# Moving a nested product's steps forward in a Strassen-type feed-forward kernel

## The chip, the cores and the metric

The kernel runs on one core of one Trainium2 chip. The metric is device time in microseconds of one execution. TensorE is called PE here, its weight loads PEld, VectorE DVE, ScalarE ACT, GpSimd POOL and SyncE SP.

## The reference

Hash attention is followed by a feed-forward block. In shapes: q, k, v are (4, 8, 768, 64) and the weights are (512, 2048) and (2048, 512).

```python
mask = q_bucket[:, :, :, None] == k_bucket[:, :, None, :]
scores = np.where(mask, scale * np.matmul(q, k.transpose(0, 1, 3, 2)), -1000000000.0)
attn = softmax(scores); x = (attn @ v), heads joined   # (3072, 512)
h = x @ w_in                                            # (3072, 2048)
g = np.maximum(h, 0.0) + alpha * np.minimum(h, 0.0)
out = g @ w_out                                         # (3072, 512)
```

The four batches of 768 tokens each go through the feed-forward block one after the other.

## The kernel before, in words

The attention of all batches comes first, in 16 pairs of heads, and prepares sums of the weights beside it. Then the feed-forward block runs for batches 0 to 3. A batch has a **stage 1** (h and g, eight blocks `ff1(b, 0)` to `ff1(b, 7)`) and a **stage 2** (out, seven blocks `ff2(b, 0)` to `ff2(b, 6)`). Both multiply by a seven-product scheme of Strassen's kind: a matrix is cut in quarters (0, 1, 2 and 21 or 12), sums and differences of quarters are made (3 to 6), and seven products of such sides, added up in the right order, give the four quarters of the result. `SIDES` and the steps of `Product.step` are numbered by product: 1 is (0, 0), 2 is (1, 1), 5 is (3, 3), 6 is (4, 4), 3 is (6, 2), 7 is (5, 5), 4 is (2, 6).

In stage 1 a block is one product scheme: PE accumulates groups in PSUM banks a, b and c, ACT copies partial sums out (`p1`, `p5`, `u1`, `u2`, `h`) or copies a start value into a bank (a "seed"), DVE adds and applies the slope, and so writes g. From batch 1 on a block is a `Rest`: its products 1, 5 and 2 are not made on their own, but come from products that are nested once more and serve four blocks at once (a **unit**; a batch has units 0 and 1, of blocks 0 to 3 and 4 to 7). The class `Inner` makes two of them, called `one` (outer product 1) and `two` (outer product 5), in the function `unit`, before the unit's first block. The class `Third` makes the nested product for outer product 2; its seven steps are spread over the blocks by the table `THIRD`, whose keys are (block in the unit, place in the block). In the profile, PE groups of `Inner` and `Third` have the line L1122 and names n: na, nb, nc belong to `one`, nd, ne, nf to `two`, n_2a, n_2b, n_2c to `Third`. A step with a or d as output works on the product's running bank. Groups of the blocks have the line L928 and names f_0a, f_0c and so on; those of stage 2 z_1a, z_1b, z_1c, by product number in `ORDER`.

What each name does in the later steps:

- `sum_g(count)` (L977) takes `count` entries from the list `g_due`, in which `finish` in `ff1` puts the four differences g3, g5, g4, g6, in that order, for the rows that are complete. Stage 2 uses g0 in its block 0, g1 in block 1, g3 in 2, g4 in 3, g2 in 4, g5 in 5 and g6 in 6. In the kernel before, rows 0 to 5 are summed in pairs of blocks (128x768), rows 6 and 7 one by one (128x384), and all of them within stage 1.
- `sum_w2` (L1334) makes the weight sums ws3 to ws6 of a stage 2 product from a loaded tile wl, `sum_g2` (L1342) the sums gs3 to gs6 of its g side. ws5 and ws6, like gs5 and gs6, have one buffer and share it with copies that `Inner` and `Third` keep.
- `sum_inner(b, u, o)` (L1091) works in batch 1 only: four sums of weights for a nested product, each stored by a POOL DMA for the later batches. `load_third` (L1073, L1083) loads them on SP.
- `load_w2` (L1302) loads wl on SP; there are two buffers, so that a load waits for the product two earlier.
- `turn_out` (L1389, L1396) transposes finished output and stores it.

PSUM: tags b and c have one bank each, shared by units, blocks and stage 2; `two_banks` has three buffers, for the a banks and some c banks. A buffer comes free when its last reader has finished. The kept copies u1 and u2 of the blocks have one buffer each too.

The order on every engine is the order in which the program is written: `do` keeps it. DMAs on SP outside of `do` may be moved by the compiler. In the loop, a block's turn begins with its product 2 (`now.step(2)`, nothing for a `Rest`), and goes on with its later products; product 1 of the next block, or for a `Rest` its products 6 and 5, comes ahead of the last product of the block before:

```python
now = after
now.step(6)
third(b1, n1, "6")
now.step(5)
before.step(4)
third(b1, n1, "4")
```

Of the kernel before, what the change touches and what calls it, by code (L numbers as in the profile page):

```python
# [407 lines left out]
def fast_path(  # L408
# [460 lines left out]
    x_m, w_m, g_m = {}, {}, {}  # L869
    H2, HK, HC = DM // 4, NI // 2, CW // 2  # L870
# [112 lines left out]
    def ff1(b, i):  # L983
        whole = b == 0

        def finish(c, t, more):
            if more is None:
                h = mid.tile([P, CW], F32, name=f"h{b}_{i}", tag="h")
                do(ACT.copy(h, t))  # L989
            else:  # L990
                h = t
                do(DVE.tensor_tensor(h, t, more, op=ALU.add))

            al = slope(i, c[0] == "2")
            m = {"11": 0, "21": 1, "22": 2, "12": 5}[c]
            do(DVE.scalar_tensor_tensor(new_g(b, m)[:, i], h, al, h, op0=ALU.mult, op1=ALU.max))  # L996
            if c == "21" and (whole or i % 2 or i > 5):
                at = slice(i if whole or i > 5 else i - 1, i + 1)
                for x in ((3, 5, 0), (5, 2, 5), (4, 2, 3), (6, 1, 4)):
                    g_due.append((b, at, *x))  # L1000
            if whole or i > 5:
                sum_g(len(g_due))
            elif c in ("12", "21"):
                sum_g(1)

        w = w_m[b * NI + i]
        kind, seeded = (Product, ("b",) if i else ()) if whole else (Rest, ("a", "c"))
        made = kind(
            f"f{b}_{i}", CW, 2, lambda m, k: w[m][:, k], lambda m, k: x_m[b, m][:, k], finish, seeded=seeded,
        )  # L1010
        if not whole:
            made.p1, made.p5 = (n_s[b, i // 4, o, i % 4 // 2][:, i % 2] for o in range(2))
        return made
# [26 lines left out]
    n_w, n_x, n_s = {}, {}, {}  # L1040
# [45 lines left out]
    def sum_inner(b, u, o):  # L1086

        if b != 1:
            return
        for m, x, op, y in ((3, 21, ALU.add, 2), (4, 3, ALU.subtract, 0), (5, 0, ALU.subtract, 21), (6, 1, ALU.subtract, 4)):  # L1090
            do(DVE.tensor_tensor(n_w[b, u, o, m], n_w[b, u, o, x], n_w[b, u, o, y], op=op))  # L1091
            nc.gpsimd.dma_start(w_n_s[u, o, :, m - 3].rearrange("p (t f) -> p t f", t=2), n_w[b, u, o, m])
# [79 lines left out]
    class Third(Inner):  # L1172

        def __init__(self, b, u):
            self.key, self.o, self.seeded = (b, u, 2), 2, True
            self.name = f"n{b}_{u}_2"
            self.ps, self.sb = {}, {}

        TAG = {"p5": "p5", "u1": "p1", "u2": "gs6"}

# [52 lines left out]
                self.slopes(1)  # L1233

    thirds = {}
    THIRD = {(0, "3"): 1, (0, "7"): 2, (1, "6"): 6, (1, "4"): 5, (1, "3"): 7, (1, "7"): 3, (2, "6"): 4}

    def third(b, i, place):

        n = THIRD.get((i % 4, place))  # L1240
        if n:
            if n == 1:
                thirds[b, i // 4] = Third(b, i // 4)
            thirds[b, i // 4].step(n)

    def unit(b, u, before):

        def bank(name, tag=None):
            name = f"n{name}{b}_{u}"
            return psum_bc[0].tile([P, 512], F32, name=name, tag=tag) if tag else two_banks(name)[:, 0]  # L1250

        one = Inner(b, u, 0, bank("a"), bank("b", "b"), bank("c"))
        one.step(1)
        one.step(5)
        before.step(4)
        one.step(2)
        if not u:
            sum_inner_x(b, 1)
        one.step(6)
        if not u:  # L1260
            sum_inner(b, 0, 1)
            sum_x(b, 3, DVE)
        two = Inner(b, u, 1, bank("d"), bank("e", "b"), bank("f", "c"))
        two.step(1)
        one.step(3)
        two.step(5)
        one.step(7)
        two.step(2)
        two.step(6)
        one.step(4)  # L1270
        two.step(3)
        now = ff1(b, 4 * u)
        now.step(1)
        two.step(7)
        now.step(6)
        now.step(5)
        two.step(4)
        if u:
            sum_w2(b, 0, 3, 4, 6, 5)
        turn_out()  # L1280
        if not u:
            sum_inner_x(b, 2)
        sum_inner(b, u, 2)
        return now

    def new_g(b, m):
# [39 lines left out]
    def sum_w2(b, n, *ms):  # L1326

        if n < 7:
            for m in ms:
                x, op, y = {  # L1330
                    3: (21, ALU.add, 2), 4: (3, ALU.subtract, 0), 5: (0, ALU.subtract, 21), 6: (1, ALU.subtract, 4),
                }[m]
                w2[b, n, m] = t = late[0].tile([P, HK, H2], F32, name=f"ws{b}_{n}_{m}", tag=f"ws{m}", bufs=1 + (m < 5))
                do(DVE.tensor_tensor(t, w2[b, n, x], w2[b, n, y], op=op))  # L1334
# [157 lines left out]
    for pi in range(NPAIR):  # L1492
        i = 2 * pi
# [93 lines left out]
    for j, (b, what, n) in enumerate(blocks):  # L1587
        n2 = n + 1 if what == "2" else 0 if n == NI - 1 else 7
        if n2 == 0:
            sides_g(b, 0)  # L1590
            if b == 0:
                sum_w2(b, 0, 3, 4)
        if not j:
            now.step(6)
        elif not (b and what == "1"):
            now.step(2)
        if j == 0:
            now.step(3)
            now.step(7)
            now.step(2)  # L1600
        if what == "2" and n == 6 and b + 1 < B:
            sum_inner(b + 1, 0, 0)
        now.step(22)
        if (b, what, n) == (1, "2", 1):
            largest()
        if what == "2" and b + 1 < B and 2 <= n < 6:
            if n == 3:
                sum_inner_x(b + 1, 0)
            else:
                sum_x(b + 1, {2: 0, 4: 1, 5: 2}[n], DVE)  # L1610
        if b and what == "1" and n == 1:
            load_inner(b, 1)
        if b and what == "1" and n == 2:
            load_third(b, 1)
        if b and what == "1" and n in (2, 3):
            sum_inner(b, 1, n - 2)
        if 0 < n2 < 7:
            sides_g(b, n2)
            sum_w2(b, n2, 3, 4)
        if n2 < 7:  # L1620
            sum_g2(b, n2, 3, 4)
        if j:
            if not (b and what == "1"):
                now.step(5)
                now.step(6)
            now.step(3)
            if b and what == "1":
                third(b, n, "3")
            if n2 or b == 0:
                sum_w2(b, n2, 6)  # L1630
            if b and what == "1" and (n + 1) % 4:
                after = ff1(b, n + 1)
                after.step(1)
            now.step(7)
            if b and what == "1":
                third(b, n, "7")
            if n2 or b == 0:
                sum_w2(b, n2, 5)
            sum_g2(b, n2, 5)
        if (b, what, n) == (1, "2", 3):  # L1640
            verdict()

        for n_out in [(), (0,), (1,), (2, 3), (4,), (5, 6), (7,)][j] if j < 7 else ():
            sum_out(n_out)
        for n_out in [(1,), (2, 3), (4,), (5, 6), (7,)][j] if j < 5 else ():
            load_out(n_out)
        if what == "1":
            load_w(b * NI + n + 3)

            if b and n in (2, 5):  # L1650
                load_w2(b, n // 4)
            if not b and n >= NI - 2:
                load_w2(b, n - NI + 2)
        else:
            load_w2(b, n + 2)
            if b + 1 < B:
                if n == 5:
                    load_inner(b + 1, 0)
                    load_third(b + 1, 0)
                if n == 0:  # L1660
                    load_x(b + 1)
        if j + 1 == len(blocks):
            turn_last(0)
        elif what == "1" or n < 6:
            turn_out()
        before = now
        if j + 1 < len(blocks):
            b1, what1, n1 = blocks[j + 1]
            if b1 and what1 == "1" and n1 % 4 == 0:
                now = unit(b1, n1 // 4, before)  # L1670
            elif b1 and what1 == "1":
# [6 lines that stand above are left out]
            else:  # L1678
                now = ff1(b1, n1) if what1 == "1" else ff2(b1, n1)
                now.step(1)  # L1680
                before.step(4)
        else:
            before.step(4)
        if n2 < 7:
            sum_g2(b, n2, 6)
# [29 lines left out]
```

## Time and profile before

| what | value |
|---|---|
| median of three runs | 870.87 us |
| range | 870.1 to 871.62 us |
| profiled execution | 870.79 us |
| its span, first to last instruction | 868.9 us |
| PE, DVE, ACT, POOL busy | 850.8, 773.6, 407.5, 154.2 us |
| granted PE clock, mean | 0.998 |

A batch's stage 1 takes about 70 us and its stage 2 about 64 us in batches 1 to 3 (stage 1 of the last batch runs from 722.5 to 792.5). PE's groups in stage 1 have four matmuls, of 384 columns (L928) or 192 (L1122), in stage 2 eight of 192. In a timeline, a row is: start in us from the start of the span, duration, engine, line, operation, out<-in with its shape, how many were merged, and in brackets the idle time before it with what ended it. Durations overlap a little with the next start, so the time that a row costs is read from start to start.

### The profile page before, as it was taken

Reading aid. Unit: us, or ns where it says so; the run is one execution under the profiler, and the core shown is the slowest. Engines: PE = TensorE matmul, PEld = TensorE weight load, DVE = VectorE, ACT = ScalarE, POOL = GpSimd, SP = SyncE. Lnnn points to the kernel's source line nnn. Section 1 sums busy time; section 2 is a strip of 40 time slices with the busy share of each in tenths; the row PEclk is TensorE's granted clock in tenths of the full one; section 3 lists DMA queues with packets and bytes.
Section 4 is the critical chain, followed back from the end, with each engine's and each line's share of the span. In section 5 each row is a group of like instructions: output and inputs, shape, how many; then the busy total and the mean of one; then the engine's idle time right before and its main releaser. Section 6 shows DMA issues by size and latency. Waiting matters only on the chain.

```text
span 868.9 us, 15379 instructions
## 1 busy us (share of the span) xinstructions
PE 850.8 (98%) x5674; PEld 598.5 (69%) x5674; DVE 773.6 (89%) x1263; ACT 407.5 (47%) x754; POOL 154.2 (18%) x321
## 2 busy tenths in 40 slices
PE   9999999999999999999999999999999999999996
PEld 4444444444444445569997768998767998677996
DVE  6999999999999977899997899996889997869886
ACT  7777888878788823321124441114442113452111
POOL 1322423333433310210015100003000001200000
PEclk9999999999999999999999999999999999999999
DMA  8856879889697537774355633444833335720242
GB/s 199 192 131 132 208 177 235 171 202 236 133 265 196 158 131 246 249 257 157 119 167 174 238 117 108 129 154 135 304 114 123 118 107 182 284 98 1 98 164 60
DMA packets 181765, 144.85 MB, mean 167 GB/s; under 512 B 121536, under 2 KB 161648, under 8 KB 178096
## 3 DMA queue, kind: packets, MB, share of 16 engines
q1 hardware_dynamic: 166496, 113.15, 45.5%
q0 software_dynamic: 12176, 29.29, 11.2%
q10 hardware_dynamic: 3008, 1.33, 0.6%
q8 instruction: 47, 0.77, 0.4%
q14 instruction: 38, 0.31, 0.1%
HBM read 111.16 MB, written 31.46 MB: 164 GB/s over the span
## 4 chain that ended last, share of the span: by engine, by line


## 5 line engine op out<-in xcount | busy, mean ns | idle before, releaser
L790 ACT ACTIVATE pt<-sc 128x768 f32<-128x768 f32 x192 | 153.9, 812 | 3.3 <-PE sc L787 3.0
L787 PE MATMUL sc<-qT,kT 64*128 64x384 f32 x768 | 155.1, 482 | 0.0
L820 PE MATMUL av<-pt,vn 128*32 128x385 f32 (+1 forms) x1536 | 127.0, 485 | 0.0
L820 PEld LDWEIGHTS av<-pt,vn 128*32 128x32 f32 x1536 | 50.3, 109 | 73.9 <-issue 69.3
L787 PEld LDWEIGHTS sc<-qT,kT 64*128 64x128 f32 x768 | 68.3, 187 | 37.7 <-issue 37.5
L1396 POOL DMA_DIRECT2D out_dram<-o x52 | 28.2, 551 | 340.6 <-DVE o L1389 339.1
L977 DVE TENSOR_TENSOR g<-g,g 128x384 f32<-128x384 f32 (+1 forms) x92 | 63.9, 710 | 1.1
L787 PE MATMUL sc<-qb,kb 64*128 64x384 bf16 x384 | 63.1, 323 | 0.8 <-DVE alpha L563 0.5
L1342 DVE TENSOR_TENSOR gs<-g,gs 128x768 f32<-128x768 f32 x56 | 53.3, 951 | 1.0
L1342 DVE TENSOR_TENSOR gs<-g 128x768 f32<-128x768 f32 x56 | 53.2, 951 | 0.0
L1334 DVE TENSOR_TENSOR ws<-wl 128x512 f32<-128x512 f32 x56 | 38.4, 685 | 7.6 <-DMA wl<-w_out_s 7.5
L787 PEld LDWEIGHTS <-kb 64*128 64x128 bf16 x384 | 19.5, 94 | 34.9 <-issue 11.9
L607 ACT ACTIVATE wr<-raw 128x512 int32<-128x512 uint32 x32 | 22.1, 691 | 30.0 <-DVE wso L651 15.2
L798 DVE TENSOR_TENSOR accp<-pt,pt 128x1536 f32<-128x1536 f32 x16 | 28.1, 1757 | 7.3 <-ACT pt L790 7.3
L748 POOL DMA_DIRECT2D qb<-hr x60 | 30.0, 506 | 25.7 <-ACT hr L743 25.7
L996 DVE SCALAR_TENSOR_TENSOR g<-h,alpha 128x384 f32<-128x384 f32 x39 | 23.9, 613 | 7.1 <-ACT h L989 7.1
L803 DVE TENSOR_TENSOR accd<-accd,pt 128x1536 f32<-128x1536 f32 x16 | 28.1, 1758 | 1.7
L809 DVE TENSOR_TENSOR accd<-accd,accp 128x1536 f32<-128x1536 f32 x16 | 28.1, 1758 | 0.6
L806 DVE TENSOR_TENSOR accp<-accp,pt 128x1536 f32<-128x1536 f32 x16 | 28.1, 1754 | 0.0
L802 DVE TENSOR_TENSOR accd<-pt,pt 128x1536 f32<-128x1536 f32 x16 | 28.0, 1751 | 0.0
L1546 ACT ACTIVATE qT<-qT 128x768 f32<-128x768 f32 x15 | 12.7, 845 | 25.8 <-DMA kb<-hr 19.0
L1354 DVE TENSOR_TENSOR m<-m,m 128x768 f32<-128x768 f32 x24 | 22.7, 946 | 0.3
(494 smaller groups left out, 1903.7 us busy)
## 6 DMA issues: line engine op xcount, KB each, us to landing
wi<-w_in_s SPq DMA_DIRECT2D x32, 512.0 KB
wl<-w_out_s SPq DMA_DIRECT2D x16, 1024.0 KB
wl<-w_out_r SPq DMA_DIRECT2D x12, 1024.0 KB
raw<-in_moe_w_in_dram POOLq DMA_DIRECT2D x15, 512.0 KB, 5.0
raw<-in_moe_w_out_dram POOLq DMA_DIRECT2D x14, 512.0 KB, 4.9
w_in_s<-wsi SPq DMA_DIRECT2D x16, 448.0 KB
qn<-in_q_dram SPq DMA_DIRECT2D x64, 96.0 KB
vn<-in_v_dram SPq DMA_DIRECT2D x16, 384.0 KB
```

Source lines behind the costliest of these rows:

```text
L748: queue.dma_start(bits[name, pi][D * s : D * s + 2 * NB, half * CW : (half + 1) * CW], raw[c : c + 2 * NB],)
L787: do(PE.matmul(sc[:, s, :CW], what["k", pi][r, ks], what["q", pi][r, qs], start=first, stop=not first,))
L790: do(ACT.activation(pts[kc][:, g, :, :CW], sc[:, :, :CW], AF.Exp, scale=SCALE / DOWN))
L798: do(DVE.tensor_tensor(accp[pi], p(0), p(1), op=ALU.add))
L803: do(DVE.tensor_tensor(accd[pi], accd[pi], p(5), op=ALU.add))
L806: do(DVE.tensor_tensor(accp[pi], accp[pi], p(2), op=ALU.add))
L809: do(DVE.tensor_tensor(accd[pi], accd[pi], accp[pi], op=ALU.add))
L820: do(PE.matmul(av[pi][D * s + t : D * s + t + 32, g, :w], nat["v", pi][:, s, kc * D + t : kc * D + t + 32], pts[kc][:, g, s, :w], start=(k ...
L977: do(DVE.tensor_tensor(new_g(b, to)[:, at], g_m[b, x][:, at], g_m[b, y][:, at], op=ALU.subtract))
L1334: do(DVE.tensor_tensor(t, w2[b, n, x], w2[b, n, y], op=op))
L1342: do(DVE.tensor_tensor(t, g2[b, n, x], g2[b, n, y], op=ALU.subtract))
L1396: pinned(b + 1 < B and queue is nc.sync, queue.dma_start(out_v[b, ch * CH + c].rearrange("(w r) d -> r w d", r=32)[:, :, cols], src[32 * a ...
```

## The change

Five edits, in the code of batches 1 to 3:

1. The `Third` object is made in `unit`, and some of its steps are called there. In unit 0, step 1 stands at the end of `unit`, ahead of the first block's product 3. In unit 1, step 1 follows `two.step(6)`, step 2 follows `two.step(3)`, and step 6 follows `two.step(4)`. `THIRD` becomes a table for each unit, with the other steps: in unit 0, step 2 moves from place "7" of the first block to place "3", where step 1 was, and the rest stay; in unit 1, steps 5 and 7 are in the first block, 3 and 4 ahead of the second.
2. `Third` gets a first `n_x` with the two unsummed quarters, since step 1 in unit 0 now stands ahead of `sum_inner_x(b, 2)`.
3. In unit 1, `sum_inner(b, 1, 2)` (batch 1) and `sum_w2(b, 0, 3, 4)` move from the end of `unit` to after `one.step(7)`; `sum_w2(b, 0, 6, 5)` stays at the end.
4. Rows 6 and 7 of g's sums are treated as a pair, and `sum_g` takes one entry at a time there too.
5. So three of the last four sums are left at the end of stage 1: `sum_g(1)` takes one in block 0 of stage 2 and `sum_g(2)` two in block 1.

The numbers and shapes of matmuls, and every DMA, are as before.

```diff
-            if c == "21" and (whole or i % 2 or i > 5):
-                at = slice(i if whole or i > 5 else i - 1, i + 1)
+            if c == "21" and (whole or i % 2):
+                at = slice(i if whole else i - 1, i + 1)
...
-            if whole or i > 5:
+            if whole:
                 sum_g(len(g_due))
             elif c in ("12", "21"):
                 sum_g(1)
...
+            n_x.setdefault((b, 2), {k: x_m[b, 1][:, k, :HC] for k in range(2)})
...
-    THIRD = {(0, "3"): 1, (0, "7"): 2, (1, "6"): 6, (1, "4"): 5, (1, "3"): 7, (1, "7"): 3, (2, "6"): 4}
+    THIRD = (
+        {(0, "3"): 2, (1, "6"): 6, (1, "4"): 5, (1, "3"): 7, (1, "7"): 3, (2, "6"): 4},
+        {(0, "3"): 5, (0, "7"): 7, (1, "6"): 3, (1, "4"): 4},
+    )
...
-        n = THIRD.get((i % 4, place))
+        n = THIRD[i // 4].get((i % 4, place))
         if n:
-            if n == 1:
-                thirds[b, i // 4] = Third(b, i // 4)
             thirds[b, i // 4].step(n)
...
         one.step(7)
+        if u:
+            sum_inner(b, 1, 2)
+            sum_w2(b, 0, 3, 4)
         two.step(2)
         two.step(6)
+        three = thirds[b, u] = Third(b, u)
+        if u:
+            three.step(1)
         one.step(4)
         two.step(3)
+        if u:
+            three.step(2)
         now = ff1(b, 4 * u)
         now.step(1)
         two.step(7)
         now.step(6)
         now.step(5)
         two.step(4)
+        three.step(6 if u else 1)
         if u:
-            sum_w2(b, 0, 3, 4, 6, 5)
+            sum_w2(b, 0, 6, 5)
         turn_out()
         if not u:
             sum_inner_x(b, 2)
-        sum_inner(b, u, 2)
+            sum_inner(b, 0, 2)
         return now
...
+        if what == "2" and n < 2:
+            sum_g(1 + n)
```

## The prediction

> **What bounds the kernel now.** I read the page, then the waits of TensorE, then the timelines of PE, DVE and ACT around each wait. The run from which all durations come took 870.79 us: a span of 868.9 and 1.9 around it, 0.08 below the median of the runs, 870.87. Three runs lie within 0.2%, so a change under 0.2% could not be told from none.
>
> From the page:
>
> ```profile
> span 868.9 us, 15379 instructions
> ...
> PE 850.8 (98%) x5674; PEld 598.5 (69%) x5674; DVE 773.6 (89%) x1263; ACT 407.5 (47%) x754; POOL 154.2 (18%) x321
> ```
>
> TensorE's own stream is the bound; time can be won only where it waits. The view of waits (total, times, longest):
>
> ```profile
> PE z_1c L928 <- DVE f_7u L992: 3.4, 3, 1.1
> PE z_2c L928 <- DVE m L1363: 1.6, 3, 0.5
> ...
> PE f_3c L928 <- ACT f_3c L1020: 1.0, 1, 1.0
> PE f_4c L928 <- ACT f_4c L1020: 0.9, 3, 0.3
> PE f_0c L928 <- ACT f_0c L1020: 0.9, 3, 0.3
> ```
>
> Four of the five come once in each of batches 1 to 3. The PE timeline, last batch, where columns are start, duration, what:
>
> ```profile
> 768.39 0.81 PE L1122 MATMUL nd<-xn,wq 128*128 128x192 f32 x4
> 769.51 1.56 PE L928 MATMUL f_4c<-x,wi 128*128 128x384 f32 x4 [0.30 <-ACT f_4c L1020]
> 770.90 0.81 PE L1122 MATMUL n_2a<-x,wt 128*128 128x192 f32 x4
> ...
> 795.06 1.46 PE L928 MATMUL z_1b<-g,wl 128*128 128x192 f32 x8
> 797.67 1.57 PE L928 MATMUL z_1c<-gs,ws 128*128 128x192 f32 x8 [1.14 <-DVE f_7u L992]
> 799.08 1.46 PE L928 MATMUL z_1a<-gs,ws 128*128 128x192 f32 x8
> ```
>
> Unhindered starts lie 0.65 us apart (n), 1.29 (f), 1.30 (z). So a wait costs more than its label: f_4c comes 0.46 late and its successor another 0.11, 0.57 together (f_0c the same); z_1c 1.31 + 0.11 = 1.42; z_2c (805.58 to 807.55 to 808.96) 0.67 + 0.11 = 0.78; f_7c (788.35 to 789.79 to 791.18), whose wait has no label, 0.15 + 0.10 = 0.25. The DVE timeline says why z_1c is late:
>
> ```profile
> 793.08 2.20 DVE L977 TENSOR_TENSOR g<-g,g 128x384 f32<-128x384 f32 x4
> 795.21 0.95 DVE L1342 TENSOR_TENSOR gs<-g 128x768 f32<-128x768 f32 x1
> 796.19 0.96 DVE L1342 TENSOR_TENSOR gs<-g,gs 128x768 f32<-128x768 f32 x1
> 797.07 0.55 DVE L992 TENSOR_TENSOR f_7u<-f_7u,f_7c 128x384 f32<-128x384 f32 x1
> ```
>
> z_1c takes f_7c's PSUM bank (tag c, one buffer), and DVE reads f_7c only after g's sums. It still trails at z_2c, which needs z_1c's bank.
>
> [...] the trace has 0.95 and 0.55, so two half sums cost more than one whole.
>
> **The change, part by part,** on the last batch's clock with its second unit starting as before. Pitches (start to start) are from the DVE rows: L992 0.58, L996 0.54, pair sum L977 0.87, L1196 0.47 (0.58 if the next needs it), slopes 1.06, gs 0.87, ws 0.61 to 0.72.
>
> *One n_2a ahead of f_0c.* No work is added; its 0.65 covers ACT's seed of bank c, which started at 734.10 and let PE go 0.54 later, 734.64; f_0c is now due at 734.83. Gain 0.57. Its own seed of bank b is done on ACT about 735.5, before n_2b at 736.1.
>
> *n_2a, n_2b, n_2a into the second unit.* PE's sum is unchanged, but f_4c is due at 770.99 and its seed comes at 770.26, so PE could go at 770.80: gain 0.57, with 0.19 to spare. New first n_2a: 765.15. Its bank is nc's, read by DVE at 763.4; its weights were issued on SP at 750.2 to 753.1 and the DMA engines fell idle at 758.7, so cover is 6 us.
>
> *DVE order in the second unit.* ws3 and ws4 (1.4 us) move into DVE's idle time after 765.1: free. In batch 1 the four sums of the third weight tile (1.5 us) come first, and their four POOL stores move with them; POOL idled 11.8 us just there. On SP, f_7's weights wait for f_4a's last group, which now ends at 778.3 for 776.9; f_7 needs them at 786.5, and a load took about 5: hidden. The next product's wl waits for na's last group, 0.65 later, and is used 33 us on: hidden. But the new n_2u addition waits for n_2a (770.34), ACT (771.19) and starts at 771.70, with ws6 and ws5 queued behind it; DVE idles from 769.7 to 771.7, where it did ws before. From there it runs without a gap: ws6 772.17, f_4u 773.38, the third product's four remaining adds and four slopes by 782.11, f_5u 782.11, its L996 782.69 to 783.31. Who waits: ACT's f_6u copy, whose one buffer is f_5u's. The trace shows this chain one step later:
>
> ```profile
> 788.87 0.48 ACT L935 COPY f_7u<-f_7a 128x384 f32<-128x384 f32 x1 [1.08 <-DVE g L996]
> 789.25 0.49 ACT L1020 COPY f_7c<-n 128x384 f32<-128x384 f32 x1
> ```
>
> L996 ended at 788.78 and PE's f_7c went at 789.79, 1.01 later. So f_6c goes at 784.32, not 783.91: **loss 0.41 + 0.10 = 0.5**. Bounds: 0 if the chain is 0.4 shorter, 1.0 if 0.5 longer.
>
> *g's sums.* Rows 6 and 7 become one pair: eight half sums (4.40) become four whole ones (3.7). One stays in stage 1, three (2.8) go into blocks 0 and 1 of stage 2. Continuing: f_6u 786.60, f_6's last L996 789.80, gs3 791.20, gs4 792.18, f_7u 793.06 to 793.6. z_1c, due at 795.53 + 0.5, waits no more: gain 1.42. f_7c: L996 ends 787.80, PE free at 788.81, due 789.57: gain 0.25. z_1c's bank is read at 802.74 to 803.1, z_2c is due at 805.1: gain 0.78.
>
> Per batch 0.57 + 0.57 + 0.25 + 1.42 + 0.78 = 3.59, less 0.5: 3.09. In three batches 9.3 us.
>
> **What is late next.** DVE now waits for DMA early in stage 2. Loads of wl leave when PE ends the product two earlier:
>
> ```profile
> 548.55 0.69 DVE L1334 TENSOR_TENSOR ws<-wl 128x512 f32<-128x512 f32 x1 [0.49 <-DMA wl<-w_out_s]
> ```
>
> That load left at 543.8: 4.75 us; 4.9 and 5.2 in the later batches. The one before it is freed by z_1a's last group (802.53, SP 804.03) and lands near 808.95, while DVE would come at 807.35. Then ws, gs, m, two moved sums (1.85), the x sum of the next batch: DVE reaches the next ws at 819.45, 7.82 after z_2a's last group against 6.39 before in batch 2, 6.25 in batch 1. So DVE trails PE by 1.4 to 1.6 more. Slack of bank c in batch 2: z_6c 1.76, z_3c 1.77, z_7c 1.85, z_4c 1.29 (with 0.26 of DMA wait to absorb): all just enough. In batch 1: z_6c 1.91, z_3c 1.92, then the verdict's small operations; z_7c 0.97, z_4c 0.42. I take waits of 0.76 and 0.55 there: **loss 1.3**, bounds 0 and 3. Batch 3 has no x sums and no wait.
>
> Sum: 9.3 - 1.3 = 8.0; 870.79 - 8.0 = **862.8 us**.
>
> **Rivals.**
> 1. *All waits vanish, no new one.* For: f_6c's delay is a difference of 0.4 in a chain of 11.6, batch 1's slack may be wider. Against: both sums come from rows that repeat within 0.05. 3 x 3.59 = 10.8: 860.0.
> 2. *DVE becomes the bound of stage 2.* For: in batch 1 its block between first m sums takes 10.55 (556.14 to 566.69) where PE needs 7 x 1.30 = 9.1. If none of the 2.8 moved is absorbed, batch 1 loses 2.8 - 0.4 = 2.4 and batch 2 about 1.5: 870.79 - 9.3 + 3.9 = 865.4. Against: DVE starts stage 2 4.4 us earlier than before (799.30 for 803.70).
> 3. *Slower: the wl load closes a loop.* A slot freed by PE, a load, the sums, bank c, PE again: z_1a's last group at 802.53 to z_5c at 814.2 is 11.7 with 1.75 of slack. A load longer than 6.6 us delays each of five blocks in three batches; from 7.3 on (0.6 x 15 = 9.3) the gain is gone, at 8 us the time is about 882 (1.35 x 15 = 20, less 9.3). Against: three measured loads within 4.75 to 5.2, and the DMA engines idle between them.
> 4. *No change*: f_4c's and z_1c's waits return elsewhere in full. Nothing in the rows is late by so much.
>
> **How the numbers follow.** My forecast (861.5 to 864.5) gets 0.50, rival 1 (859.5 to 861.5) 0.20, rival 2 (864.5 to 869) 0.19, rival 3 0.06, no change 0.05. The range 859.8 to 866.8 leaves out the slower end of rival 2, rivals 3 and 4. Faster 0.89, same 0.05, slower 0.06.
>
> **What would show it.** Right: no wait at f_0c, f_4c, z_1c, z_2c; f_3c's 1.0 in batch 1 still there; a new wait of 0.3 to 0.4 at f_6c in each batch, ACT's f_6u behind DVE's L996; DVE idle about 2 us before the n_2u addition of the second unit, and about 1.6 for wl in block 1 of stage 2; in batch 1 short waits at z_7c or z_4c. Wrong: bank c waits through stage 2 in batches 1 and 2, an n_2a waiting for wt, or transfers placed otherwise on SP.

## The result and the profile after

The changed kernel took 862.74 us (median of four runs, 862.27 to 863.08) beside 871.25 for the kernel before, measured beside it (870.1 to 871.68): a ratio of 0.9904, 95% interval 0.9887 to 0.9921. It is faster by about 1%, and the interval lies clear of 1. The forecast was 862.8.

The profiled execution of the changed kernel took 862.93 us, with a span of 861.1. Its page, first part:

```profile
span 861.1 us, 15383 instructions
...
PE 848.1 (98%) x5674; PEld 598.6 (70%) x5674; DVE 770.9 (90%) x1251; ACT 407.7 (47%) x754; POOL 154.5 (18%) x321
```

PE has its 5674 matmuls as before, DVE twelve instructions fewer: in three batches, eight half sums became four whole ones. In the kernel before, a half sum (128x384, 56 of them) took 0.555 us on the mean and a whole one (128x768, 36) 0.952; in the changed kernel it is 0.554 (32) and 0.951 (48). The view of PE's waits (total, times, longest; its other rows stand ahead of batch 1's first f_0a, and all but nf's 0.4 belong to the attention part):

```profile
PE f_3c L928 <- ACT f_3c L1020: 1.0, 1, 1.0
...
PE f_6c L928 <- ACT f_6c L1020: 0.8, 3, 0.3
...
PE z_7a L928 <- DMA wl<-w_out_s: 0.4, 1, 0.4
...
PE z_4c L928 <- DVE m L1374: 0.2, 1, 0.2
```

The four rows that came three times each, at f_0c, f_4c, z_1c and z_2c, are gone. One new row comes three times (f_6c); two new ones come once, both in batch 1. The PE timeline of the last batch; its second unit starts 5.11 us earlier than before (752.25 for 757.36), so a time of the kernel before less 5.11 is the same point ("on the new clock" below):

```profile
765.23 0.81 PE L1122 MATMUL n_2a<-xn,wt 128*128 128x192 f32 x4
765.88 1.45 PE L928 MATMUL f_4c<-x,wi 128*128 128x384 f32 x4
767.17 0.81 PE L1122 MATMUL n_2c<-xn,wt 128*128 128x192 f32 x4
...
777.51 1.45 PE L928 MATMUL f_5a<-x,wi 128*128 128x384 f32 x4
779.22 1.56 PE L928 MATMUL f_6c<-x,wi 128*128 128x384 f32 x4 [0.25 <-ACT f_6c L1020]
780.62 1.45 PE L928 MATMUL f_6a<-x,wi 128*128 128x384 f32 x4
...
789.65 1.46 PE L928 MATMUL z_1b<-g,wl 128*128 128x192 f32 x8
790.96 1.46 PE L928 MATMUL z_1c<-gs,ws 128*128 128x192 f32 x8
```

f_4c stands 0.65 behind the n_2a that now precedes it, z_1c 1.31 behind z_1b: both at the unhindered distance, with no wait. f_6c, due at 777.51 + 1.29 = 778.80, is 0.42 late, and its successor comes after 1.40 instead of 1.29, another 0.11: 0.53 in all.

The time can be counted by batch, from the start of a batch's first f_0a to that of the next one (of the last batch, to the last transposition of its output), in us of the profiled executions:

| kernel | first f_0a of batch 1 | batch 1 | batch 2 | batch 3 |
|---|---|---|---|---|
| before | 459.10 | 137.27 | 135.87 | 128.77 |
| after | 459.55 | 135.36 | 132.79 | 125.71 |
| gain | -0.45 | 1.91 | 3.08 | 3.06 |

The batches give 8.05. The attention part ended 0.45 later in this execution, and the end behind the last transposition is 0.20 shorter (7.69 for 7.89): 8.05 - 0.45 + 0.20 = 7.80, the difference of the spans, 868.9 - 861.1.

### The profile page after: what moved, and what is told of

The parts are those of the page before. It is cut to its first block, busy times and chain, and to the rows that moved or that the text cites. A ratio compares the mean times of both kernels' runs of the same rounds, so it can differ in the third digit from the quotient of the medians.

```text
span 861.1 us, 15383 instructions
## 1 busy us (share of the span) xinstructions
PE 848.1 (98%) x5674; PEld 598.6 (70%) x5674; DVE 770.9 (90%) x1251; ACT 407.7 (47%) x754; POOL 154.5 (18%) x321
## 3 DMA queue, kind: packets, MB, share of 16 engines
q10 hardware_dynamic: 3008, 1.33, 0.6%
## 4 chain that ended last, share of the span: by engine, by line
## 5 line engine op out<-in xcount | busy, mean ns | idle before, releaser
L977 DVE TENSOR_TENSOR g<-g,g 128x768 f32<-128x768 f32 (+1 forms) x80 | 62.7, 792 | 0.7
L996 DVE SCALAR_TENSOR_TENSOR g<-h,alpha 128x384 f32<-128x384 f32 x39 | 23.9, 613 | 6.4 <-ACT h L989 6.4
```

Of the source, the lines that this page charges most:

```text
L977: do(DVE.tensor_tensor(new_g(b, to)[:, at], g_m[b, x][:, at], g_m[b, y][:, at], op=ALU.subtract))
```

## The experiments

All are read by the same table of batch lengths. The start of batch 1 moved between 458.86 and 460.65 from one execution to another though nothing before it was edited, so that a difference under 1 us shows in the batches and not in the medians. Most of this is attention (batch 0's first f_0a came between 312.48 and 313.59); batch 0 itself took 146.37 or 146.38 us in every trace but e4's.

| kernel | time, us | first f_0a of batch 1 | batch 1 | batch 2 | batch 3 |
|---|---|---|---|---|---|
| e1_sums_only | 865.0 | 459.20 | 136.34 | 133.68 | 126.58 |
| e2_steps_only | 866.57 | 459.79 | 135.75 | 134.35 | 127.25 |
| e3_f0_undone | 864.51 | 459.57 | 136.11 | 133.38 | 126.29 |
| e4_pairs_stage1 | 866.4 | 460.65 | 135.68 | 134.27 | 127.17 |
| e5_ws_ahead | 861.99 | 459.31 | 135.00 | 132.55 | 125.45 |
| e6_verdict_late | 860.54 (one run) | 458.86 | 134.13 | 132.80 | 125.83 |
| e7_stores_pool | 863.07 (one run) | 459.79 | 135.61 | 132.80 | 125.70 |
| e8_all_three | 860.95 | 459.87 | 133.83 | 132.54 | 125.57 |
| e9_inner_later | 859.29 | 459.30 | 132.55 | 132.55 | 125.57 |
| e10_after_again | 862.71 | 459.97 | 135.32 | 132.81 | 125.70 |

### The two halves of the change: e1, e2, e3

**e1_sums_only** is the kernel before with the edits of g's sums alone.

```diff
-            if c == "21" and (whole or i % 2 or i > 5):
-                at = slice(i if whole or i > 5 else i - 1, i + 1)
+            if c == "21" and (whole or i % 2):
+                at = slice(i if whole else i - 1, i + 1)
...
-            if whole or i > 5:
+            if whole:
                 sum_g(len(g_due))
...
+        if what == "2" and n < 2:
+            sum_g(1 + n)
```

> The kernel before with the two edits on g's sums alone (rows 6 and 7 as a pair, three sums in stage 2). Ledger of PE waits: z_1c's 1.42 and z_2c's 0.78 go in each batch, f_0c, f_4c (0.57 each) and f_7c (0.25) stay, no wait at f_6c; batch 1 loses about 1.2 in its stage 2 as the changed kernel does. 6.6 - 1.2 = 5.4: 865.4 us. Rival, that the steps of the nested product bring most: under 2 us, above 868.5.

Measured: 865.0 us (864.55 to 865.61), ratio to the kernel before 0.9935 (0.9918 to 0.9951). Of its view of PE's waits:

```profile
PE f_0c L928 <- ACT f_0c L1020: 0.9, 3, 0.3
PE f_4c L928 <- ACT f_4c L1020: 0.9, 3, 0.3
PE z_7a L928 <- DMA wl<-w_out_s: 0.4, 1, 0.4
...
PE z_4c L928 <- DVE m L1363: 0.3, 1, 0.3
```

z_1c and z_2c are free, f_0c and f_4c wait as before, and the two rows of batch 1 are there. So these two come with g's sums in stage 2, not with the steps of the nested product. Batches 2 and 3 gain 2.19 each.

**e2_steps_only** is the other half: the changed kernel with g's sums as before.

```diff
-            if c == "21" and (whole or i % 2):
-                at = slice(i if whole else i - 1, i + 1)
+            if c == "21" and (whole or i % 2 or i > 5):
+                at = slice(i if whole or i > 5 else i - 1, i + 1)
...
-            if whole:
+            if whole or i > 5:
                 sum_g(len(g_due))
...
-        if what == "2" and n < 2:
-            sum_g(1 + n)
```

> The changed kernel with g's sums as before, so the moved steps and weight sums alone. Ledger: f_0c and f_4c gain 0.57 each, f_7c 0.25, f_6c loses 0.52; z_1c still waits, 0.77 in place of 1.42, z_2c as before; no wait in batch 1's stage 2. 1.5 in each batch, 4.6 in all: 866.2 us. Rival, that the sums bring everything: 870.5 or more.

Measured: 866.57 us (866.09 to 867.03), ratio 0.995 (0.9933 to 0.9967). Of its view of PE's waits:

```profile
PE z_2c L928 <- DVE m L1374: 1.6, 3, 0.5
PE z_1c L928 <- DVE f_7u L992: 1.5, 3, 0.5
...
PE f_6c L928 <- ACT f_6c L1020: 0.8, 3, 0.3
```

f_6c's wait belongs to the moved steps. z_1c still waits for f_7's sums, 0.5 each time instead of 1.1. Counted from the start of the last batch's unit 1, DVE starts f_7u 0.95 earlier than in the kernel before (793.20 - 754.44 = 38.76 for 797.07 - 757.36 = 39.71), while PE comes due at z_1c 0.29 earlier (0.57 + 0.25 - 0.53). So the moved steps and weight sums also take 0.66 of z_1c's 1.42; which of them does it was not tested. Batches 2 and 3 gain 1.52 each. With e1's 2.19 that is 3.71 for the 3.08 and 3.06 of both halves together: about that 0.66 is counted in both. Nothing waits in batch 1's stage 2.

**e3_f0_undone** puts the first n_2a of unit 0 back behind f_0c, all else changed.

```diff
-        {(0, "3"): 2, (1, "6"): 6, (1, "4"): 5, (1, "3"): 7, (1, "7"): 3, (2, "6"): 4},
+        {(0, "3"): 1, (0, "7"): 2, (1, "6"): 6, (1, "4"): 5, (1, "3"): 7, (1, "7"): 3, (2, "6"): 4},
...
-        three.step(6 if u else 1)
+        if u:
+            three.step(6)
```

> The changed kernel, but in unit 0 the first n_2a stands behind f_0c again. Ledger: f_0c waits 0.3 on its label, 0.57 with its successor, in three batches: 1.7 slower than the changed kernel, 864.5 us. Rival, that some other engine sets the pace there: no difference, 862.8.

Measured: 864.51 us (863.77 to 865.46), ratio 0.9925 (0.9909 to 0.9942). f_0c's wait is back:

```profile
PE f_0c L928 <- ACT f_0c L1020: 0.9, 3, 0.3
PE z_7a L928 <- DMA wl<-w_out_s: 0.8, 1, 0.8
```

Batches 2 and 3 are 0.59 and 0.58 longer than in the changed kernel. The step was put at 0.57. In batch 1 it is 0.75, with a longer wait at z_7a: z_7a and z_4c cost 1.33 there with their successors, for 1.16 in the changed kernel.

### Where the sums stand: e4

Pairs, as in the change, but all four sums at the end of stage 1.

```diff
-            if whole:
+            if whole or c == "21" and i == 7:
                 sum_g(len(g_due))
...
-        if what == "2" and n < 2:
-            sum_g(1 + n)
```

> The changed kernel with rows 6 and 7 as a pair, but all four of their sums at the end of stage 1. Ledger: z_1c still free; 2.6 us of sums stand ahead of z_1c's reader, which had 1.55 to spare, so z_2c waits 1.1 and loses 1.2 in each batch; batch 1 wins its 1.16 in stage 2 back: 3 x 1.2 - 1.2 = 2.4 slower than the changed kernel, 865.2 us. Rival, that the pairing (0.7 us less of DVE in each batch) is what counts and the place isn't: 862.8 or less.

Measured: 866.4 us (865.94 to 867.57), ratio 0.9948 (0.9931 to 0.9965). Of its waits:

```profile
PE z_2c L928 <- DVE m L1374: 2.3, 3, 0.8
...
PE z_1a L928 <- DVE gs L1353: 0.5, 3, 0.2
```

DVE is again late at the start of stage 2, though the pairs are cheaper than the half sums (0.95 us for one whole sum, 1.11 for two halves). Batches 2 and 3 are 1.48 and 1.46 longer than in the changed kernel; 1.2 was expected. The wait at z_1a, for a sum of g's side, had not been foreseen. z_1c has no row: beside the moved steps the pairing is enough to free it, as row 6's sums no longer stand ahead of f_7c's reader. But the wait moves on to z_1a and z_2c: beside e2, with half sums in the same place, batches 2 and 3 are only 0.08 shorter. So making pairs is not enough; the place of the sums in stage 2 frees z_2c and brings the 1.48 and 1.46. In batch 1 the two waits of its stage 2 are gone, and the cost is only 0.32. The profiled execution, 867.57, is the longest of the four. In it batch 0, which the edit leaves as it was, took 148.07 us for 146.38: z_4a waited 1.0 there for a load of wl that left SP at 433.18, 7.48 us before z_4a started.

### What f_6c waits for: e5

The sums ws6 and ws5 go ahead of step 6 of the nested product, so that DVE makes them while it would idle.

```diff
         two.step(4)
-        three.step(6 if u else 1)
         if u:
             sum_w2(b, 0, 6, 5)
+        three.step(6 if u else 1)
```

> The changed kernel, but in unit 1 DVE makes ws6 and ws5 ahead of the n_2u addition, in the 2 us in which it stood idle. Ledger: f_5u's L996 ends 1.2 us earlier, f_6c's wait (0.52 in each batch) goes, nothing else moves since the load of wl sets DVE's pace in stage 2: 1.6 faster than the changed kernel, 861.2 us. Rival, that DVE is the bound from there on: its whole 1.3 to 2 us in each batch, 857 to 859.

Measured: 861.99 us (861.91 to 862.55), ratio 0.9901 (0.9885 to 0.9918). Batches 2 and 3 gain 0.24 and 0.26, not 0.52. The DVE timeline of the changed kernel:

```profile
766.60 0.56 DVE L1197 TENSOR_TENSOR g<-n_2u,n 128x384 f32<-128x384 f32 x1 [2.03 <-ACT n_2u L1186]
767.07 0.68 DVE L1345 TENSOR_TENSOR ws<-wl,ws 128x512 f32<-128x512 f32 x1
767.67 0.68 DVE L1345 TENSOR_TENSOR ws<-wl 128x512 f32<-128x512 f32 x1
...
777.60 0.62 DVE L996 SCALAR_TENSOR_TENSOR g<-f_5u,alpha 128x384 f32<-128x384 f32 x1
```

And of e5_ws_ahead, where unit 1 of the last batch, and so the same points, lie 0.84 earlier (751.41 for 752.25):

```profile
764.36 0.68 DVE L1345 TENSOR_TENSOR ws<-wl 128x512 f32<-128x512 f32 x1
765.75 0.56 DVE L1197 TENSOR_TENSOR g<-n_2u,n 128x384 f32<-128x384 f32 x1 [0.71 <-ACT n_2u L1186]
766.53 0.55 DVE L992 TENSOR_TENSOR f_4u<-f_4u,f_4c 128x384 f32<-128x384 f32 x1 [0.22 <-PE f_4c L928]
...
771.06 0.56 DVE L1197 TENSOR_TENSOR g<-n_2c,g 128x384 f32<-128x384 f32 x1 [0.40 <-PE n_2c L1122]
...
776.50 0.62 DVE L996 SCALAR_TENSOR_TENSOR g<-f_5u,alpha 128x384 f32<-128x384 f32 x1
```

The 2.03 of idle time shrinks to 0.71, and the two sums are out of the chain. But DVE then reaches f_4's and n_2c's groups before PE has ended them and waits 0.22 and 0.40. L996 of f_5u starts 1.10 earlier (776.50 for 777.60), of which 0.84 is the offset and only 0.26 is gained. f_6c is 0.16 + 0.11 late instead of 0.42 + 0.11. DVE's order sets the wait, and behind it stand PE's own groups.

### Batch 1: e6, e7, e8, e9, e10

The PE timeline of the changed kernel in batch 1's stage 2:

```profile
564.50 1.46 PE L928 MATMUL z_3a<-gs,ws 128*128 128x192 f32 x8
566.35 1.57 PE L928 MATMUL z_7a<-g,wl 128*128 128x192 f32 x8 [0.39 <-DMA wl<-w_out_s]
567.76 1.46 PE L928 MATMUL z_3a<-gs,wl 128*128 128x192 f32 x8
...
578.16 1.46 PE L928 MATMUL z_4b<-g,wl 128*128 128x192 f32 x8
579.85 1.57 PE L928 MATMUL z_4c<-gs,ws 128*128 128x192 f32 x8 [0.23 <-DVE m L1374]
```

z_7a is 0.55 late (566.35 - 564.50 - 1.30) and z_4c 0.39, each with 0.11 more at its successor: 1.16. z_7a waits for its weights. SP's timeline of the kernel before, around the load of these weights:

```profile
555.41 5.55 SPq L1396 DMA_DIRECT2D out_dram<-o  x12
562.11 0.68 SPq L1302 DMA_DIRECT2D wl<-w_out_s  x1
```

And of the changed kernel, where they come late:

```profile
550.27 0.32 SPq L1313 DMA_DIRECT2D wl<-w_out_s  x1
554.32 7.11 SPq L1407 DMA_DIRECT2D out_dram<-o  x12
561.52 0.38 SPq L1313 DMA_DIRECT2D wl<-w_out_s  x1
```

The load's slot is freed by z_6a's last group. Before, that group ended at 562.08 and the load left at 562.11. After, it ended at 559.46, but SP was issuing twelve stores of finished output until 561.43: the load left 2.06 late. Two causes were thus open for batch 1's loss: SP's stores, or DVE's lag, in which the small operations of the verdict (`largest` and `verdict`, which reduce the largest values to a flag) stand in batch 1 alone.

**e6_verdict_late** moves those operations to batch 3.

```diff
-        if (b, what, n) == (1, "2", 1):
+        if (b, what, n) == (3, "2", 1):
             largest()
...
-        if (b, what, n) == (1, "2", 3):
+        if (b, what, n) == (3, "2", 3):
             verdict()
```

> The changed kernel with the small DVE operations of the verdict (1.7 us, and one transpose on PE) moved from batch 1 to the same blocks of batch 3. Read from PE's milestones in batch 1, not from the time: z_4c's wait (0.50 with its successor) goes; z_7a's (0.66), which waits for wl behind SP's output stores, stays. Rival, that both are DVE's lateness: both go, 1.2. Batch 3 pays nothing in either.

Measured in a single run: 860.54 us. Batch 1 is 134.13, 1.23 shorter than in the changed kernel; both its waits are gone. Of this 0.11 is the transpose on PE, which went along, and batch 3 pays 0.12 for it. The expectation that z_7a's would stay was wrong: the twelve stores took 6.29 here, the load left at 559.95 and landed in time. As the stores were shorter too, the comparison that tells is the one with e10, below.

**e7_stores_pool** leaves DVE alone and moves eight of the twelve stores to POOL's queue, in batches 0 to 2.

```diff
-                    queue = nc.gpsimd if (... or b + 1 < B and c and p in (5, 4)) else nc.sync
+                    queue = nc.gpsimd if (... or b + 1 < B and c and p in (5, 4, 2)) else nc.sync
```

> The changed kernel with two thirds of the output stores of z_2 (the 12 on SP in front of a load of wl in blocks 2 of stage 2) issued on POOL. z_7a's wait for wl in batch 1 goes (0.66), but z_7c, whose bank DVE frees at the same time as before, waits about 0.6 in its place, and z_4c's 0.5 stays: no gain in batch 1's stage 2. Rival, that the load alone cost the 0.66: batch 1's stage 2 is 0.66 shorter.

Measured in a single run: 863.07 us. Its SP timeline in batch 1:

```profile
554.82 1.79 SPq L1407 DMA_DIRECT2D out_dram<-o  x4
559.75 0.34 SPq L1313 DMA_DIRECT2D wl<-w_out_s  x1
```

And its PE timeline there:

```profile
570.68 1.57 PE L928 MATMUL z_7c<-gs,ws 128*128 128x192 f32 x8 [0.57 <-DVE m L1374]
```

The stores are done before the slot comes free, and z_7a's wait is gone, but batch 1 is 135.61, no shorter than 135.36. In its place z_7c waits for DVE: 0.73 late and 0.11 more, and z_4c 0.46 and 0.10. So mending the load brings nothing here: DVE's lag is behind it, and in the changed kernel the late load only shows it three groups sooner. Where the load is later still it costs more, as in e3, where z_7a started 5.6 us after the load left (561.78 to 567.39) and not 4.8, and batch 1 lost 0.17 more.

**e8_all_three** has e5, e6 and e7 together.

```diff
-        three.step(6 if u else 1)
         if u:
             sum_w2(b, 0, 6, 5)
+        three.step(6 if u else 1)
...
+        if (b, what, n) == (3, "2", 3):
             verdict()
...
+                    queue = nc.gpsimd if (... or b + 1 < B and c and p in (5, 4, 2)) else nc.sync
```

> The changed kernel with the weight sums ahead, the verdict in batch 3 and the stores on POOL. If the ledger adds up: 1.6 from f_6c and 1.2 from batch 1's stage 2, 2.8 faster than the changed kernel, 860.0 us, and no PE wait left from batch 1 on but f_3c's 1.0 in batch 1. Rival, that waits only change places: 861 or more, with new waits in stage 2.

Measured: 860.95 us (860.33 to 861.63), ratio 0.9885 (0.9869 to 0.9902). The three batches take 391.94 in all, 1.92 less than in the changed kernel (393.86). From batch 1's first f_0a on PE has one labelled wait, f_3c's 1.0 in batch 1, which stood before the change too. The 860.0 expected was missed mostly by what f_6c keeps, 0.27 in each batch, 0.8 in all.

**e9_inner_later** is e8 with batch 1's weight sums for unit 1, made in blocks 2 and 3, moved behind place "7" of these blocks, to free DVE ahead of f_3c.

```diff
-        if b and what == "1" and n in (2, 3):
-            sum_inner(b, 1, n - 2)
...
             if b and what == "1":
                 third(b, n, "7")
+            if b and what == "1" and n in (2, 3):
+                sum_inner(b, 1, n - 2)
```

> All three edits of the run before, and in batch 1 the weight sums of blocks 2 and 3 (1.5 us of DVE each) behind the block's product 7 in place of ahead of its product 3. Ledger: bank c of f_2c is read 1.5 us earlier, f_3c's wait (1.28 with its successor) goes: batch 1 takes 132.55 us from f_0a to f_0a in place of 133.83, no labelled PE wait is left after unit 0's front in batch 1, 859.7 us. Rival, that the same DVE work only delays the next reader: a wait of about 1 at a group of unit 1's front, 860.7 us or more.

Measured: 859.29 us (858.56 to 860.81), ratio 0.9872 (0.9857 to 0.9887). Batch 1 is 132.55, as expected, and as long as batch 2. The view of PE's waits ends with:

```profile
PE nf L1122 <- DVE wp L1091: 0.4, 1, 0.4
PE sc L787 <- ACT pt L790: 0.3, 1, 0.3
PE sc L787 <- DVE alpha L563: 0.2, 1, 0.2
```

The `sc` rows, and one row ahead of these three, are of the attention part. nf's wait is in batch 1's first unit, at 454.65, ahead of its first f_0a, and every kernel here has it. After that no row is left. This version is faster than both kernels: on the same chip the changed kernel took 862.71.

**e10_after_again** is that: the changed kernel with no edit.

> The changed kernel again, on the same chip beside the run before: 862.7 us, batches of 135.4, 132.8 and 125.7 us; the attention part in front of them may start up to 1 us earlier or later in one execution.

Measured: 862.71 us (862.29 to 865.88), ratio 0.9918 (0.9903 to 0.9932). Of its waits:

```profile
PE z_4c L928 <- DVE m L1374: 0.3, 1, 0.3
PE z_7c L928 <- DVE m L1374: 0.3, 1, 0.3
```

z_7a does not wait here, z_7c does; the stores took 6.29 us, and batch 1 is 135.32 for 135.36. The same kernel shows either label for the same loss.

## Why the prediction was right, and where it was off

**Right in time and cause.** The batches were put at gains of 1.79, 3.09 and 3.09, and measured 1.91, 3.08 and 3.06. e3 shows the step at f_0c (0.59 and 0.58 for 0.57); e1 and e2 part the two halves, and the waits stand where the steps put them. f_4c's gain was not undone on its own: it waits in e1 and not in e2, where the other moved steps are in too. That the median met the forecast within 0.1 us is in part luck, as the start of batch 1 alone moves by more than that from one execution to the next.

- *One n_2a ahead of f_0c* and *n_2a, n_2b, n_2a into the second unit*: both waits are gone, and neither wt nor SP's moved loads stopped PE. f_7c's small wait is gone too.
- *DVE order in the second unit*: DVE was to start the n_2u addition at 771.70 after 2.0 of idle time, which is 766.59 on the new clock; it started at 766.60 after 2.03. L996 of f_5u was to end at 783.31, or 778.20; it ended at 778.22. f_6c lost 0.53 for 0.5. ACT's side of this chain:

```profile
778.30 0.48 ACT L935 COPY f_6u<-f_6a 128x384 f32<-128x384 f32 x1 [1.40 <-DVE g L996]
778.68 0.49 ACT L1020 COPY f_6c<-n 128x384 f32<-128x384 f32 x1
```

  f_6u's copy waits for L996, and PE goes at 779.22, 1.00 after L996's end; 1.01 was taken from f_7c's row.
- *g's sums*: z_1c and z_2c free. e4 shows that the pairing frees z_1c but alone wins only 0.08 (beside e2), and that moving the sums into stage 2 brings the rest. The mechanism held; e4's own size, 1.2, was 1.5, the difference mostly z_1a's wait.
- *f_3c* kept its 1.0, as said.

**The step that failed: What is late next, in batch 1.** The sum was nearly right, 1.16 for 1.3. The place was not: waits were put at z_7c and z_4c, both for DVE; in the profiled execution they stood at z_7a, for the wl load, and at z_4c. The wrong premise was that loads of wl leave when PE ends the product two earlier. It leaves out SP's own queue. Ahead of this load stand the twelve stores of block 1's output, whose issue ended 1.1 us ahead of the slot's release before the change (555.41 + 5.55 = 560.96, for 562.08), and 2.0 us behind it after the change. PE released the slot 2.62 earlier, the stores started only 1.09 earlier, and their issue took 1.56 longer. The premise did little harm to the sum, as e7 and e10 show: with the load in time, the predicted waits appear, and the batch is about as long (135.61 and 135.32 for 135.36). e6 shows DVE to be the cause: without the verdict's operations, 1.39 us of DVE between 562.36 and 563.75, batch 1 is 1.19 shorter than in e10 (134.13 for 135.32), where the stores took the same 6.29; 0.11 of this is PE's transpose.

**Two sizes off.** DVE was to wait 1.6 for wl in block 1 of stage 2. It waited 0.84 in the last batch, 0.75 in batch 2 and 0.69 in batch 1:

```profile
803.68 0.69 DVE L1345 TENSOR_TENSOR ws<-wl 128x512 f32<-128x512 f32 x1 [0.84 <-DMA wl<-w_out_s]
```

The load took 4.73 (798.95 to 803.68) for the 4.9 assumed, which is the small part. The larger one is that DVE came later. In the sum DVE ran without a gap from f_6u to f_7u, while f_6c's delay of 0.5 had been charged to PE alone. It reaches DVE too: f_6's last slope waits 0.49 for ACT's copy h of f_6a, whose last group comes behind f_6c:

```profile
784.09 0.62 DVE L996 SCALAR_TENSOR_TENSOR g<-n,alpha 128x384 f32<-128x384 f32 x1
785.20 0.62 DVE L996 SCALAR_TENSOR_TENSOR g<-h,alpha 128x384 f32<-128x384 f32 x1 [0.49 <-ACT h L989]
...
788.46 0.55 DVE L992 TENSOR_TENSOR f_7u<-f_7u,f_7c 128x384 f32<-128x384 f32 x1
```

f_7u was to start at 793.06, or 787.95 on the new clock; it started 0.51 later. z_1c had room for it: it went at 790.96, and it was due, f_6c's delay included, at 790.92.

**The rivals.** Rival 1 (no new wait) fell at f_6c and in batch 1. Rival 2 (DVE bounds stage 2) came true in batch 1 at half its size, 1.16 for 2.4, and not in batch 2, where nothing waits in stage 2. Rival 3, a loop closed through the wl load, did not appear: one load in one batch was late. (Its 0.6 x 15 is 9.0, not 9.3; the forecast does not use it.) Rival 4, no change, is excluded by the interval.

## What to carry to other kernels

A wait on the bounding engine that repeats can be priced to a tenth of a microsecond from start-to-start distances, the successor's loss included (0.57 at f_0c, for 0.59 and 0.58 in e3). The next wait can be found by following the new order instruction by instruction through every engine of the chain; its size is less sure (0.53 for 0.5 at f_6c and 1.16 for 1.3 in batch 1, but 1.48 for 1.2 in e4 and a gain of 0.25 for 0.52 in e5). A delay that is charged to one engine has to be carried on to those that read from it: f_6c's, charged to PE, was a wait of 0.49 on DVE too. For a load, look at what stands ahead of it in its own queue as well as at what frees its slot (twelve stores held this one for 2.06); and before mending the wait that has the label, ask what would wait next: in batch 1 mending the load gave nothing (135.61 for 135.36), and taking work from DVE gave all of it (134.13).

## What the runs showed of the hardware

The issue of the same twelve stores on SP in batch 1 took 5.55 us before the change and 5.56 in e2 and e4, and 6.29 (e6 and e10), 6.49 (e5), 6.78 (e3), 7.00 (e1) and 7.11 us in the changed kernel; in batch 2 it was 5.55 to 5.59 in every kernel that issues all twelve on SP. Two executions of one kernel, the changed one, had 7.11 and 6.29. The excess is in a single store. In the changed kernel eleven of the twelve took 0.34 to 0.43 us, and one this:

```profile
558.02 1.98 SPq L1407 DMA_DIRECT2D out_dram<-o  x1
```

The place of g's sums is not the reason: in the last batch the twelve took 6.43 us in the kernel before and 7.04 in e4, both without sums in stage 2, and 5.56 in e3, which has them. The traces show what such a store coincides with. The view of DMA queues lists 47 packets of 16 KB of the kind `instruction` in an execution, and in each of the six executions with a long store in batch 1 one of them starts within 0.25 us of that store (558.18 in the changed kernel). Before the change, in e2 and in e4 this packet came only with the last of the twelve stores or behind it. The last batch shows the same: 832.81 for the long store at 832.84 in the kernel before, and in e3 a packet at 827.66, as the twelfth store ends. Over all twelve traces, from 410 us on, 43 of the 44 SP issues that took over 0.9 us start within 0.35 us of such a packet; in the kernel before it is 4 of 4, in the changed kernel 4 of 5. No run moved these packets, so that they are the cause is not shown.
